# Attention loop of a fused network kernel: the next tile's scores moved directly behind the output products

## The chip, the core and the metric

The kernel runs on one core of a Trainium2 chip. The core has five engines with an instruction stream each, and each runs its stream strictly in the order in which it was written: TensorE (PE, matrix products and transpositions), VectorE (DVE), ScalarE (ACT), GpSimd (POOL) and SyncE (SP, which here issues transfers). They wait for each other through semaphores. The metric is the device time of one execution in microseconds; lower is better. The two levels of TensorE's clock are 1.2 and 2.4 GHz; a granted clock of 1.00 in the profile is 2.4 GHz.

## What is computed

Three layers in a row, all in 32-bit floating point: windowed attention, a mixture of eight experts whose choice of expert runs along the sequence, and a gated two-layer product. Only the first is touched by the change:

```python
def _attn_ref(q, k, v, n_global, n_local):          # (2, 8, 768, 64): batch, heads, sequence, head size
    ...
    scores = scale * np.matmul(q, k.transpose(0, 1, 3, 2))
    keep = is_global | is_local                      # 8 first keys, and the last 96
    scores = np.where(keep, scores + bias[None, :, :, :], -1000000000.0)
    a = np.exp(scores - np.max(scores, axis=-1, keepdims=True))
    a = a / (np.sum(a, axis=-1, keepdims=True) + 1e-09)
    return np.matmul(a, v)
```

The attention output x then meets a small matrix (512 x 9) that gives the routing logits; from them comes, token by token, an expert, and the token's place in that expert's rows.

## The kernel before

**Tiles and iterations.** Attention goes over 12 tiles of 128 queries (6 for each of the two batches), all 8 heads at a time. A tile t is two iterations i = 2t + g of the loop at line 1149, one for each half g of the heads (four heads, as two pairs). A query tile meets 232 keys (128 of its own, 96 before them, 8 global ones); the first tile of a batch meets only its own 128. The order in which the statements stand in the loop is the order on every engine: there is no scheduler.

**The steps of one half i**, with the names by which the text calls them:

- *turns of k and q* (`turn4`, line 854, called by `emit_kT` and `emit_qT`): TensorE transposes the next tile's keys and queries (4 + 4 transpositions) into the two `S` banks; ScalarE evicts them at L862 (into `strip`, a part of the tile `zbig`) and at L866 (into `qz`). Once for each tile, in its even iteration.
- *scores* (`emit_S`, L900): TensorE multiplies `qz` and `strip`. Both halves of tile t + 1 are done in the odd iteration of tile t. The even half goes into the two `S` banks, the odd half into the banks `T` and `O`.
- *minimum* (`emit_min`, L914): VectorE adds the bias table, writes the result into one of the buffers `peb` and takes the row's minimum, four instructions for each half.
- *exponentials* (`emit_exp`, L926): ScalarE, four for each half, in place in `peb`.
- *probability transposes* (`emit_pT`, L933 and L935): TensorE, eight for each half, four into each of the two `PT` banks.
- their *evictions* (`emit_ev`): the first bank by VectorE (L944), the second by ScalarE (L942).
- *output products* (`emit_pv`, L958): both halves of a tile together at the end of the next even iteration, into an `O` bank.
- *x transposes* (`emit_xT`, L963, ScalarE, then `turn_x`, L185, TensorE, then `route_x`, L189, VectorE): the finished tile's output is turned back into rows and scaled.

**The order before.** An odd iteration has on TensorE: probability transposes of the half before, scores of both halves of the next tile, x transposes. An even iteration has: probability transposes of the half before, turns of k and q, output products.

**Routing** goes through the loop in groups of two tiles, by a table `plan` filled by `at(iteration, point, step)` and emptied by `do(i, point)`. The points lie, in the order before: `Ra` behind the probability transposes, `Dm` before the scores, `Rb` behind the x transposes or the turns of k and q, `Db` behind the minimum, `Rc` and `Dc` behind the output products. The steps that the text speaks of are TensorE's *logits* (L203 to L211, and L223 for turning them), *rows* (L263: four transpositions of the tile `ab` that VectorE makes with the chain L228 to L253), *turn* (L282, behind a scan on VectorE, L274), *sum* (L299 and L303), and the two ranking products L347 and L367. Later in the loop the first expert's weights are split in halves by ScalarE (L659) and VectorE (L664) from two points of each iteration, both named `bg_early`.

**Banks.** `S`, `O` and `PT` have two banks each, `T` and `R` one.

Behind the loop come one last half, expert 0 whose products fill TensorE while routing ends, the experts 1 to 7, and the third layer.

Of the kernel before, what the change touches and what calls it, by code (L numbers as in the profile page):

```python
# [9 lines left out]
F32 = mybir.dt.float32  # L10
# [7 lines left out]
P = 128  # L18
B, H, S, HD = 2, 8, 768, 64
D, E, F = 512, 8, 1024  # L20
NT = S // P
NTT = B * NT
# [27 lines left out]
NI = 2 * NTT  # L50
# [6 lines left out]
class Net:  # L57
# [121 lines left out]
        self.slow = c.tile([1, 1], F32, name="slow1")  # L179
        nc.vector.tensor_reduce(self.slow, slow, axis=AX.X, op=ALU.max)  # L180

    def turn_x(self, xT, t):
        self.xp = self.bank("PT", 2)
        for kk in range(KD):
            self.nc.tensor.transpose(self.xp[:, kk * P:(kk + 1) * P], xT[:, kk, :], self.ident)  # L185

# [424 lines left out]
def build(ctx, tc, ins, out):  # L611
    n = Net(ctx, tc, ins, out)
# [241 lines left out]
    def turn4(src):  # L854
        ps = n.bank("S", 2)
        for p in range(PAIRS):
            nc.tensor.transpose(ps[:, p * P:(p + 1) * P], src[:, 2 * p:2 * p + 2, :].rearrange("p a d -> p (a d)"), n.ident)
        return ps.rearrange("p (a c) -> p a c", a=PAIRS)

    def emit_kT(t):  # L860
        psv = turn4(kn.pop(t))
        nc.scalar.activation(out=strip[:, :, cols(t):cols(t) + P], in_=psv, func=ACTF.Copy)  # L862

    def emit_qT(t):
        psv = turn4(qn.pop(t))
        nc.scalar.activation(out=qz[t % 2], in_=psv, func=ACTF.Copy, scale=-1.0 / HD ** 0.5)  # L866

    def first_half(g):
# [35 lines left out]
    def emit_min(i):  # L904
        t, g = divmod(i, 2)
        N = width(t)
        if g == 0:
            stat[t] = (ap.tile([P, H], F32, tag="nm", bufs=3, name=f"nm{t}"), ap.tile([P, H], F32, tag="sm", bufs=3, name=f"sm{t}"))
        tb = n.tb if t % NT else n.tb0
        for b in range(2):  # L910
            for a in range(2):
                h = 4 * g + 2 * b + a
                pe = peb[(4 * i + 2 * b + a) % len(peb)]
                nc.vector.tensor_tensor_reduce(out=pe[:, 2 * P - N:2 * P], in0=Ss[i][a][:, b * N:(b + 1) * N], in1=tb[:, h, :], scale=1.0,  # L914
                                               scalar=3.0e38, op0=ALU.add, op1=ALU.min, accum_out=stat[t][0][:, h:h + 1])
                Pt[i, b, a] = pe
        del Ss[i]
# [81 lines left out]
    def at(i, point, *fs):  # L999
        plan.setdefault((i, point), []).extend(fs)  # L1000

    def do(i, point):
        for f in plan.pop((i, point), ()):
            f()
# [8 lines left out]
    for g in groups:  # L1013
        i = 2 * g[-1] + 3
        lgg, mx, mx2, rows, scan, tn, oh, sm_, ps_, acc = (lambda f=f, g=g: f(ap2, g) for f in (
            lambda _, g: n.route_lgt(ap2, g, xTs), n.route_max, n.route_max2, n.route_rows, n.route_scan, n.route_turn, n.route_oh, n.route_sum,
            lambda _, g: pos(g), n.route_acc))
        if g[-1] == NTT - 1:
            tail = mx, mx2, rows, scan, tn, oh, sm_, ps_
            continue  # L1020
        at(i, "Rb", lgg)
        at(i + 1, "E0", lambda g=g: n.route_lge(ap2, g))
        at(i + 1, "Rb", lambda g=g: n.route_lgb(ap2, g))
        at(i + 1, "Db", mx, mx2)
        if g[-1] == NTT - 3:
            tail8 = rows, scan, tn, oh, sm_, ps_, acc
            continue
        at(i + 1, "Rc", rows)
        if g[-1] == NTT - 5:
            at(i + 1, "Dc", scan)  # L1030
            at(i + 2, "Ra", tn)
            at(i + 2, "Dm", oh)
            at(i + 2, "Rb", sm_)
            at(i + 2, "Db", ps_, acc)
        else:
            at(i + 2, "Dm", scan)
            at(i + 2, "Rb", tn)
            at(i + 2, "Db", oh)
            at(i + 3, "Rb", sm_)
            at(i + 3, "Db", ps_, acc)  # L1040
        if g[-1] in (5, 7):
            e = g[-1] == 7
            at(i + 3 - e, "Db", lambda e=e: n.order_a(ap2, "fg"[e], n.cnte if e else n.cnt6, n.fvec if e else None))
            if e:
                at(i + 3, "Rb", n.order_k)
                at(i + 3, "Db", lambda: n.order_c(ap2, "g", rp))
            else:
                at(i + 3, "Dc", lambda: n.order_b(ap2, "f", rp))
            at(i + 4, "Ra", lambda e=e: n.early_pick(rp, 3 * e))
            at(i + 4, "Dm", lambda e=e: early_start(3 * e, e))  # L1050

    with tc.manual_schedule():
# [3 lines left out]
            load("q", 0, g)  # L1056
        n.setup()
        peb = [ap.tile([P, 2 * P], F32, name=f"peb{i}") if i % 2 else zflat[:, i // 2, S:S + 2 * P] for i in range(8)]
        qzz = ap.tile([P, 2 * PAIRS * P], F32, name="qz")
        qz = [qzz[:, i * D:(i + 1) * D].rearrange("p (a c) -> p a c", a=PAIRS) for i in range(2)]  # L1060
        glob = ap.tile([P, PAIRS, NG], F32, name="glob")
# [86 lines left out]
        tq.pop(0)()  # L1148
        for i in range(NI - 1):
            t, g = divmod(i, 2)  # L1150
            if 0 < i:
                emit_pT(i - 1, 0)
                emit_pT(i - 1, 1)
            do(i, "Ra")
            emit_exp(i, 0)
            do(i, "E0")
            if 0 < i:
                emit_ev(i - 1, 0)
            if i > 1 and g == 1:
                emit_xT(t - 1)  # L1160
            if 0 < i:
                emit_ev(i - 1, 1, True)
            emit_exp(i, 1)
            if i and g == 0:
                n.route_ri(t - 1, stat[t - 1][1])
            do(i, "Dm")
            bg_early()
            if i == 1:
                n.routing_consts()
            ahead = [] if i and not g else [u for u in (i + 1, i + 2) if u < NI and u // 2 == (i + 1) // 2]  # L1170
            for u in ahead:
                emit_S(u)
            for u in ahead:
                if u // 2 % NT < NT - 1:
                    emit_kglob(u)
            if i == 0:
                emit_kglob(0)
            if scq:
                scatter(scq.pop(0))
            if g == 0 and t + 1 < NTT:  # L1180
                emit_kT(t + 1)
                if t + 2 < NTT:
                    load("k", t + 2)
                emit_qT(t + 1)
                if t + 2 < NTT:
                    load("q", t + 2)
            if g == 1 and i > 1:
                n.turn_x(xTs[t - 1], t - 1)
            do(i, "Rb")
            bg_early()  # L1190
            if i < NI - 2:
                emit_min(i + 1)
            if g == 1 and i > 1:
                if t - 1 == XW[0]:
                    n.xw = wp.tile([P, 2 * D], F32, tag="whi", bufs=9, name="xw")
                n.route_x(ap, X, t - 1)
            do(i, "Db")
            for u in (i - 2, i - 1) if i and not g else ():
                emit_pv(u, 0)
                emit_pv(u, 1)  # L1200
            do(i, "Rc")
            do(i, "Dc")
            for _ in scq[:2]:
                scatter(scq.pop(0))
            if g == 1 and t + 2 < NTT:
                load("v", t + 2)
            if g == 0 and 0 < t and (t + 1) % NT and t + 1 < NTT:
                load_vp(t + 1)
            if 0 < i <= E // 2:
                for e in (2 * i - 2, 2 * i - 1):  # L1210
                    nc.scalar.dma_start(out=n.xs[e * REG:e * REG + PRE, :], in_=n.warm)
            if tq:
                for _ in range(NTAB[i]):
                    if tq:
                        tq.pop(0)()
                if not tq:
                    tstack.close()
                    n.counters(ap)
                    dp = astack.enter_context(tc.tile_pool(name="dp", bufs=1, reuse_waits="tile"))
                    dwa = dp.tile([P, 1024], F32, name="dwa")  # L1220
            if i == 3:
                n.gate_rest()
                n.mix_load()
            if i == 4:
                n.mix_rest()
                n.limits(n.const)
            if 0 in wsrc and early is None:
                early = True
                ld_q = list(range(4))
                hi_q = [None] * 3 + [(c, s_) for c in range(NIN) for s_ in range(2)]  # L1230
                bg_early()
            if i in (4, 11, 17):
                dec_load(PIECES[(4, 11, 17).index(i)], dwa)
            if i in (7, 13):
                dgen = dec(PIECES[i // 13], word_tile)
            if i in (7, 8, 9, 13, 14, 15):
                next(dgen, None)
            if i == NI - 2:
                dec_load(PIECES[3], qzz)
# [11 lines left out]
        i = NI - 1  # L1251
# [44 lines left out]
        g = groups[-1]  # L1296
# [710 lines left out]
```

## Time and profile before

| what | before |
|---|---|
| time, median of 3 runs (lowest, highest) | 482.1 us (479.89, 483.13) |
| the profiled execution | 480.05 us, of which 478.2 us are the span from the first to the last instruction |
| granted TensorE clock, mean over the span | 0.999 |
| busy in the span: TensorE, VectorE, ScalarE, GpSimd | 461.2, 344.4, 266.8, 116.4 us |
| the loop's steady part, from tile 1 to tile 11 | 16.78 to 100.67 us, 83.89 us |

In the rows below a time is counted from the start of the span. A matmul's row gives its start, its modelled length, engine, line, out<-in, shape and count; in brackets stand the idle time ahead of it and what ended that. Matmuls overlap: one of 128 columns is shown as 0.27 us long, and the next can start 0.11 us after it started. So a pause on TensorE is read from starts.

### The profile page before, as it was taken

The page shows a single profiled execution, that of the slowest core. Times are in us where ns is not written, and L with a number is a line of the kernel's source. Part 1 is how long each engine was busy: PE and PEld are TensorE (multiplying, and loading weights), DVE is VectorE, ACT ScalarE, POOL GpSimd, SP SyncE. Part 2 cuts the span into 40 slices and gives each one's busy share as a digit, 9 for nine tenths or more (in the row PEclk, how much of TensorE's full clock was granted, in tenths as well). Part 3 has the DMA queues.
Part 4 walks back from the last instruction along what each step waited for, and adds up shares of the span by engine and source line. Part 5 has one row for each costly group of instructions (what it writes and reads, how often), then busy time and mean ns, then how long its engine had stood idle before and what let it go on. Part 6 is the DMA issues. An engine that isn't in the chain of part 4 may idle for free. (4 is left out here: it accounts for less than half of the span.)

```text
span 478.2 us, 9266 instructions
## 1 busy us (share of the span) xinstructions
PE 461.2 (96%) x3210; PEld 396.0 (83%) x3210; DVE 344.4 (72%) x911; ACT 266.8 (56%) x657; POOL 116.4 (24%) x200
## 2 busy tenths in 40 slices
PE   7999999999999999999999999999999999999995
PEld 5787878777788989879879877897989898898984
DVE  6868797896858866987898888797848767363301
ACT  4877877984427735567686686852424324152320
POOL 4112202202300000000010013061844819162220
PEclk9999999999999999999999999999999999999999
DMA  8986486796576886698699743003737451200001
GB/s 193 281 221 165 129 197 185 226 282 217 184 259 203 315 276 253 219 334 311 220 356 377 246 149 111 23 1 118 280 111 265 144 177 53 88 1 23 23 3 49
DMA packets 76491, 86.90 MB, mean 182 GB/s; under 512 B 50676, under 2 KB 50932, under 8 KB 76436
## 3 DMA queue, kind: packets, MB, share of 16 engines
q1 hardware_dynamic: 68176, 63.01, 41.7%
q0 software_dynamic: 4944, 17.17, 10.9%
q10 hardware_dynamic: 3316, 6.03, 3.4%
q8 instruction: 28, 0.46, 0.4%
q14 instruction: 27, 0.22, 0.1%
HBM read 73.49 MB, written 12.71 MB: 180 GB/s over the span
## 5 line engine op out<-in xcount | busy, mean ns | idle before, releaser
L659 ACT ACTIVATE whi<-wraw 128x512 fp32r<-128x512 f32 x128 | 72.5, 623 | 6.5 <-ACT yo L778 2.2
L668 DVE TENSOR_TENSOR wlo<-wraw,whi 128x1024 fp32r<-128x1024 f32 x55 | 66.1, 1218 | 2.4 <-ACT whi L659 2.2
L1518 ACT ACTIVATE sq<-S 128x256 f32<-128x256 f32 x48 | 18.5, 385 | 73.1 <-PE S L677 70.9
L675 PE MATMUL S<-xkh,whi 128*128 128x256 f32 x192 | 54.4, 283 | 0.2 <-ACT whi L659 0.2
L1528 POOL TENSOR_TENSOR kl<-sq,kh 128x256 fp32r<-128x256 f32 x40 | 36.5, 922 | 69.7 <-issue 36.6
L677 PE MATMUL S<-xkh,wlo 128*128 128x256 f32 x192 | 53.3, 277 | 0.2 <-DVE wlo L664 0.2
L676 PE MATMUL S<-xkl,whi 128*128 128x256 f32 x192 | 53.2, 277 | 0.0
L1558 DVE TENSOR_TENSOR o<-O,sig 128x512 f32<-128x512 f32 (+1 forms) x13 | 8.4, 650 | 51.0 <-PE O L677 31.8
L676 PE MATMUL O<-wlo,kh 128*128 128x512 f32 (+1 forms) x104 | 39.2, 377 | 0.6 <-DVE wlo L664 0.6
L677 PE MATMUL O<-whi,kl 128*128 128x512 f32 (+1 forms) x104 | 39.2, 377 | 0.0
L675 PE MATMUL O<-whi,kh 128*128 128x512 f32 (+1 forms) x104 | 38.8, 373 | 0.0
L675 PEld LDWEIGHTS S<-xkh,whi 128*128 128x128 f32 x192 | 36.1, 188 | 0.8 <-ACT whi L659 0.4
L677 PEld LDWEIGHTS S<-xkh,wlo 128*128 128x128 f32 x192 | 36.1, 188 | 0.4 <-DVE wlo L664 0.4
L676 PEld LDWEIGHTS S<-xkl,whi 128*128 128x128 f32 x192 | 36.1, 188 | 0.2
L1519 DVE SCALAR_TENSOR_TENSOR sq<-S,sq 128x256 f32<-128x256 f32 x48 | 20.1, 421 | 15.8 <-ACT sq L1518 15.5
L1527 ACT ACTIVATE kh<-sq 128x256 fp32r<-128x256 f32 x48 | 19.7, 412 | 12.9 <-DVE sq L1519 12.9
L676 PEld LDWEIGHTS O<-wlo,kh 128*128 128x128 f32 x104 | 19.6, 188 | 4.9 <-DVE wlo L664 1.0
L926 ACT ACTIVATE zbig<-zbig,nm 128x232 f32<-128x232 f32 (+1 forms) x48 | 22.4, 466 | 1.7 <-DVE nm L914 0.9
L675 PEld LDWEIGHTS O<-whi,kh 128*128 128x128 f32 x104 | 19.6, 188 | 3.7
L677 PEld LDWEIGHTS O<-whi,kl 128*128 128x128 f32 x104 | 19.6, 188 | 3.5 <-DVE kl L1528 0.2
L926 ACT ACTIVATE peb<-peb,nm 128x232 f32<-128x232 f32 (+1 forms) x48 | 22.2, 464 | 0.0
L307 POOL DMA_INDIRECT xs<-X,posi x10 | 11.4, 1143 | 36.8 <-DVE acc L325 16.7
(466 smaller groups left out, 1407.1 us busy)
## 6 DMA issues: line engine op xcount, KB each, us to landing
wraw<-in_moe_w_dram SPq DMA_DIRECT2D x64, 512.0 KB, 5.3
dwt<-in_moe_w_v_dram POOLq DMA_DIRECT2D x8, 512.0 KB, 4.6
z<-in_moe_w_k_dram SPq DMA_DIRECT2D x8, 512.0 KB, 4.1
z<-in_moe_w_v_dram SPq DMA_DIRECT2D x8, 512.0 KB, 5.0
ys<-yo ACTq DMA_DIRECT2D x13, 256.0 KB, 7.7
vn<-in_v_dram SPq DMA_DIRECT2D x12, 256.0 KB, 3.8
xn<-xs SPq DMA_DIRECT2D x12, 256.0 KB, 4.7
dwt<-in_moe_w_k_dram POOLq DMA_DIRECT2D x6, 512.0 KB, 6.7
```

The source lines that it names most:

```text
L307: self.nc.gpsimd.indirect_dma_start(self.xviews[t], bass.IndirectOffsetOnAxis(ap=self.posi[:, t:t + 1], axis=0), X[t], None)
L659: nc.scalar.activation(out=whl[r, c][0][:, sl], in_=raws[r, c][:, sl], func=ACTF.Copy)
L668: nc.vector.tensor_tensor(lo, raws.pop((r, c)), hi.bitcast(F32), op=ALU.subtract)
L675: nc.tensor.matmul(out_, lhsT=ah, rhs=bh, start=first, stop=False)
L676: nc.tensor.matmul(out_, lhsT=ah, rhs=bl, start=False, stop=False)
L677: nc.tensor.matmul(out_, lhsT=al, rhs=bh, start=False, stop=last)
L926: nc.scalar.activation(out=pe, in_=pe, func=ACTF.Exp, scale=-1.0, bias=nm[:, h:h + 1], accum_out=sm[:, h:h + 1])
L1518: nc.scalar.activation(out=sq_, in_=ps[:, 0:TB], func=ACTF.Relu)
L1519: nc.vector.scalar_tensor_tensor(sq_, ps[:, 0:TB], 0.0, sq_, op0=ALU.max, op1=ALU.mult)
L1527: nc.scalar.activation(out=hh, in_=sq_, func=ACTF.Copy)
L1528: (nc.gpsimd if b else nc.vector).tensor_tensor(hl, sq_, hh.bitcast(F32), op=ALU.subtract)
L1558: nc.vector.tensor_tensor(o[:, a:z], ps[:, 0:z - a], sig[b, i][:, a:z], op=ALU.mult)
```

## The change

- The iterations behind the first tile whose g is 1 (`late`) have another order. The scores of the next tile now stand first, directly behind the output products that end the iteration before. ScalarE's eviction of x and the exponentials follow, the routing point `Ra`, then the probability transposes, then the x transposes; VectorE's minimum stands ahead of the point `Dm` and of the evictions.
- The even iterations put the turns of k and q ahead of the probability transposes (`turned`). Their evictions by ScalarE stay behind the exponentials.
- The x transposes go into an `O` bank instead of a `PT` bank, except in the last odd iteration.
- `peb` has twelve buffers instead of eight, so that the even halves of odd tiles have four of their own; the four new ones lie in the two tiles `exh` and `exl` and are cleared at their edge by four more GpSimd memsets (L1079).
- The routing step *rows* moves from behind the output products (`Rc` of i + 1) to `Ra` of the iteration behind it, for all groups but the one that ends with tile 7.

The first rows are TensorE's, from the end of the output products of tile 4 on. Names: `O_909` and `O_915` are the bank of these products, `S_`, `T_` and `O_962`, `O_939` take the scores of tile 6, `R_` is the routing bank, `PT_` the bank of the probability transposes. Before:

```order
L958 MATMUL O_909<-pt_1_866,vp 64x128 x2
L263 MATMUL R_926<-ident,ab_899 1x128 x4
L933 MATMUL PT_933<-ident,zbig 128x128
...
L935 MATMUL PT_938<-ident,peb_106 128x128
L900 MATMUL S_955<-zbig,qz 128x128
...
L900 MATMUL O_962<-zbig,qz 128x128
L185 MATMUL PT_971<-ident,xT_947 128x128 x4
L282 MATMUL R_976<-ones_r,er_953 128x8 x2
L933 MATMUL PT_991<-ident,zbig 128x128
```

With the change, from the same products on:

```order
L958 MATMUL O_915<-pt_1_880,vp 64x128 x2
L900 MATMUL S_932<-zbig,qz 128x128
...
L900 MATMUL O_939<-zbig,qz 128x128
L263 MATMUL R_954<-ident,ab_905 1x128 x4
L933 MATMUL PT_961<-ident,peexh 128x128
...
L935 MATMUL PT_966<-ident,peexl 128x128
L185 MATMUL O_971<-ident,xT_948 128x128 x4
L282 MATMUL R_988<-ones_r,er_982 128x8 x2
L857 MATMUL S_997<-ident,kn_889 128x128 x4
L857 MATMUL S_1002<-ident,qn_892 128x128 x4
L933 MATMUL PT_1007<-ident,zbig 128x128
```

The scores moved from behind eight probability transposes (and behind *rows*) to directly behind the output products, *rows* and the probability transposes follow them, and the turns of k and q (L857) now stand ahead of the next probability transposes instead of behind them.

The second place is ScalarE in the even iteration that belongs to these products. Before:

```order
L218 ACTIVATE lgt_862<-R_830 128x256
L942 ACTIVATE pt_1_866<-PT_855 128x512
L926 ACTIVATE zbig,sm_840<-zbig,nm_839 128x232
L926 ACTIVATE peb_106,sm_840<-peb_106,nm_839 128x232
L862 ACTIVATE zbig<-S_872 128x4x128
L866 ACTIVATE qz<-S_880 128x512
L266 ACTIVATE br_931<-R_926 1x256
```

With the change:

```order
L218 ACTIVATE lgt_878<-R_842 128x256
L942 ACTIVATE pt_1_882<-PT_871 128x512
L926 ACTIVATE peexl,sm_833<-peexl,nm_832 128x232 x2
L862 ACTIVATE zbig<-S_856 128x4x128
L866 ACTIVATE qz<-S_861 128x512
L963 ACTIVATE xT_948<-O_915 128x512
```

Up to the eviction into `qz` nothing moved here: the eviction of the second `PT` bank (L942), two exponentials, `strip`, `qz`. Behind it the eviction of x (L963) now comes first.

The diff:

```diff
@@ -179,8 +179,8 @@
         self.slow = c.tile([1, 1], F32, name="slow1")
         nc.vector.tensor_reduce(self.slow, slow, axis=AX.X, op=ALU.max)
 
-    def turn_x(self, xT, t):
-        self.xp = self.bank("PT", 2)
+    def turn_x(self, xT, t, tag="PT"):
+        self.xp = self.bank(tag, 2)
         for kk in range(KD):
             self.nc.tensor.transpose(self.xp[:, kk * P:(kk + 1) * P], xT[:, kk, :], self.ident)
 
@@ -857,12 +857,12 @@
             nc.tensor.transpose(ps[:, p * P:(p + 1) * P], src[:, 2 * p:2 * p + 2, :].rearrange("p a d -> p (a d)"), n.ident)
         return ps.rearrange("p (a c) -> p a c", a=PAIRS)
 
-    def emit_kT(t):
-        psv = turn4(kn.pop(t))
+    def emit_kT(t, psv=None):
+        psv = turn4(kn.pop(t)) if psv is None else psv
         nc.scalar.activation(out=strip[:, :, cols(t):cols(t) + P], in_=psv, func=ACTF.Copy)
 
-    def emit_qT(t):
-        psv = turn4(qn.pop(t))
+    def emit_qT(t, psv=None):
+        psv = turn4(qn.pop(t)) if psv is None else psv
         nc.scalar.activation(out=qz[t % 2], in_=psv, func=ACTF.Copy, scale=-1.0 / HD ** 0.5)
 
     def first_half(g):
@@ -910,7 +910,7 @@
         for b in range(2):
             for a in range(2):
                 h = 4 * g + 2 * b + a
-                pe = peb[(4 * i + 2 * b + a) % len(peb)]
+                pe = peb[4 * (1 if g else t % 2 * 2) + 2 * b + a]
                 nc.vector.tensor_tensor_reduce(out=pe[:, 2 * P - N:2 * P], in0=Ss[i][a][:, b * N:(b + 1) * N], in1=tb[:, h, :], scale=1.0,
                                                scalar=3.0e38, op0=ALU.add, op1=ALU.min, accum_out=stat[t][0][:, h:h + 1])
                 Pt[i, b, a] = pe
@@ -1025,14 +1025,15 @@
         if g[-1] == NTT - 3:
             tail8 = rows, scan, tn, oh, sm_, ps_, acc
             continue
-        at(i + 1, "Rc", rows)
         if g[-1] == NTT - 5:
+            at(i + 1, "Rc", rows)
             at(i + 1, "Dc", scan)
             at(i + 2, "Ra", tn)
             at(i + 2, "Dm", oh)
             at(i + 2, "Rb", sm_)
             at(i + 2, "Db", ps_, acc)
         else:
+            at(i + 2, "Ra", rows)
             at(i + 2, "Dm", scan)
             at(i + 2, "Rb", tn)
             at(i + 2, "Db", oh)
@@ -1056,6 +1057,9 @@
             load("q", 0, g)
         n.setup()
         peb = [ap.tile([P, 2 * P], F32, name=f"peb{i}") if i % 2 else zflat[:, i // 2, S:S + 2 * P] for i in range(8)]
+        for tg in ("exh", "exl"):
+            more = ap.tile([P, 4 * P], F32, tag=tg, bufs=2, name="pe" + tg)
+            peb += [more[:, 0:2 * P], more[:, 2 * P:4 * P]]
         qzz = ap.tile([P, 2 * PAIRS * P], F32, name="qz")
         qz = [qzz[:, i * D:(i + 1) * D].rearrange("p (a c) -> p a c", a=PAIRS) for i in range(2)]
         glob = ap.tile([P, PAIRS, NG], F32, name="glob")
@@ -1148,49 +1152,68 @@
         tq.pop(0)()
         for i in range(NI - 1):
             t, g = divmod(i, 2)
-            if 0 < i:
+            late = g == 1 and i > 1
+            ahead = [] if i and not g else [u for u in (i + 1, i + 2) if u < NI and u // 2 == (i + 1) // 2]
+
+            def scores():
+                for u in ahead:
+                    emit_S(u)
+                for u in ahead:
+                    if u // 2 % NT < NT - 1:
+                        emit_kglob(u)
+                if i == 0:
+                    emit_kglob(0)
+
+            turned = []
+            if late:
+                scores()
+                emit_xT(t - 1)
+                emit_exp(i, 0)
+                emit_exp(i, 1)
+                do(i, "Ra")
                 emit_pT(i - 1, 0)
                 emit_pT(i - 1, 1)
-            do(i, "Ra")
-            emit_exp(i, 0)
-            do(i, "E0")
-            if 0 < i:
+                n.turn_x(xTs[t - 1], t - 1, "O" if i < NI - 3 else "PT")
+                if i < NI - 2:
+                    emit_min(i + 1)
+                do(i, "Dm")
                 emit_ev(i - 1, 0)
-            if i > 1 and g == 1:
-                emit_xT(t - 1)
-            if 0 < i:
                 emit_ev(i - 1, 1, True)
-            emit_exp(i, 1)
-            if i and g == 0:
-                n.route_ri(t - 1, stat[t - 1][1])
-            do(i, "Dm")
+            else:
+                if i and t + 1 < NTT and not g:
+                    turned = [turn4(kn.pop(t + 1)), turn4(qn.pop(t + 1))]
+                if 0 < i:
+                    emit_pT(i - 1, 0)
+                    emit_pT(i - 1, 1)
+                do(i, "Ra")
+                emit_exp(i, 0)
+                do(i, "E0")
+                if 0 < i:
+                    emit_ev(i - 1, 0)
+                    emit_ev(i - 1, 1, True)
+                emit_exp(i, 1)
+                if i and g == 0:
+                    n.route_ri(t - 1, stat[t - 1][1])
+                do(i, "Dm")
             bg_early()
             if i == 1:
                 n.routing_consts()
-            ahead = [] if i and not g else [u for u in (i + 1, i + 2) if u < NI and u // 2 == (i + 1) // 2]
-            for u in ahead:
-                emit_S(u)
-            for u in ahead:
-                if u // 2 % NT < NT - 1:
-                    emit_kglob(u)
-            if i == 0:
-                emit_kglob(0)
+            if not late:
+                scores()
             if scq:
                 scatter(scq.pop(0))
             if g == 0 and t + 1 < NTT:
-                emit_kT(t + 1)
+                emit_kT(t + 1, *turned[0:1])
                 if t + 2 < NTT:
                     load("k", t + 2)
-                emit_qT(t + 1)
+                emit_qT(t + 1, *turned[1:2])
                 if t + 2 < NTT:
                     load("q", t + 2)
-            if g == 1 and i > 1:
-                n.turn_x(xTs[t - 1], t - 1)
             do(i, "Rb")
             bg_early()
-            if i < NI - 2:
+            if i < NI - 2 and not late:
                 emit_min(i + 1)
-            if g == 1 and i > 1:
+            if late:
                 if t - 1 == XW[0]:
                     n.xw = wp.tile([P, 2 * D], F32, tag="whi", bufs=9, name="xw")
                 n.route_x(ap, X, t - 1)
```

## Rows read from the trace of the kernel before

**Rows 1.** Stages: us, length, busy time (count) of each engine, granted clock, DMA share, GB/s

```profile
16.78:100.67 83.89, 79.51 (x885) 66.36 (x884) 68.30 (x313) 68.73 (x225) 15.45 (x34) 1.00 0.75 202
100.67:478.20 377.53, 368.17 (x2241) 320.19 (x2239) 263.32 (x522) 188.22 (x399) 93.82 (x123) 1.00 0.51 176
90.00:100.00 10.00, 8.99 (x115) 7.30 (x114) 9.83 (x37) 9.38 (x30) 2.59 (x3) 1.00 0.66 207
```

**Rows 2.** Waits of TensorE, 13 to 101 us: idle us in total, times, longest

```profile
PE PT L933 <- DVE X L189: 1.3, 3, 0.5
PE R L367 <- ACT peb L926: 0.7, 1, 0.7
PE R L263 <- DVE eq L239: 0.6, 1, 0.6
PE R L263 <- DVE ab L253: 0.5, 2, 0.3
PE R L263 <- DVE ab L242: 0.4, 2, 0.2
PE R L282 <- DVE er L274: 0.4, 1, 0.4
PE R L347 <- DVE dgf L339: 0.2, 1, 0.2
```

**Rows 3.** Timeline of TensorE over a tile without routing steps

```profile
16.78 0.33 PE L933 MATMUL PT<-ident,zbig 128*128 128x128 f32 x1
...
17.80 1.05 PE L900 MATMUL S<-zbig,qz 64*128 64x232 f32 x8
...
19.57 0.66 PE L185 MATMUL PT<-ident,xT 128*128 128x128 f32 x4
...
21.47 0.27 PE L935 MATMUL PT<-ident,peb 128*128 128x128 f32 x1
21.58 0.60 PE L857 MATMUL S<-ident,kn 128*128 128x128 f32 x4
...
22.55 0.44 PE L958 MATMUL O<-pt,vn 128*64 128x128 f32 x4
...
24.45 0.33 PE L933 MATMUL PT<-ident,zbig 128*128 128x128 f32 x1
```

**Rows 4.** Timeline of ScalarE over the same tile

```profile
21.84 0.60 ACT L942 ACTIVATE pt<-PT 128x512 f32<-128x512 f32 x1 [0.96 <-PE PT L935]
...
23.76 0.59 ACT L866 ACTIVATE qz<-S 128x512 f32<-128x512 f32 x1
```

**Rows 5.** Timeline of ScalarE and TensorE at the first scores of tile 1

```profile
11.00 0.60 ACT L866 ACTIVATE qz<-S 128x512 f32<-128x512 f32 x1
...
11.74 1.05 PE L900 MATMUL S<-zbig,qz 64*128 64x232 f32 x8 [0.41 <-ACT qz L866]
```

**Rows 6.** Timeline of TensorE: *sum*, turned logits, and the output products behind them

```profile
63.66 1.09 PE L958 MATMUL O<-pt,vn 128*64 128x128 f32 x16
...
71.78 0.26 PE L299 MATMUL R<-OH,tri 128*128 128x16 f32 x1
...
72.41 0.44 PE L958 MATMUL O<-pt,vn 128*64 128x128 f32 x4
...
80.54 0.38 PE L223 MATMUL R<-ident,lgt 128*128 128x128 f32 x2
80.86 0.44 PE L958 MATMUL O<-pt,vn 128*64 128x128 f32 x4
```

**Rows 7.** Timeline of TensorE: the step behind *rows*, after the products of 80.86

```profile
83.72 0.27 PE L933 MATMUL PT<-ident,zbig 128*128 128x128 f32 x1
```

**Rows 8.** Timeline of ScalarE: a weight split ahead of the evictions of k and q

```profile
90.90 0.62 ACT L659 ACTIVATE whi<-wraw 128x512 fp32r<-128x512 f32 x1
```

**Rows 9.** Timeline of TensorE: the turns of k and q of tile 2

```profile
14.52 0.66 PE L857 MATMUL S<-ident,kn 128*128 128x128 f32 x4 [0.35 <-DVE nm L914]
```

**Rows 10.** Timeline of GpSimd: its step behind the memsets of L1079

```profile
5.85 0.32 POOL L593 TENSOR_SCALAR tb<-d 128x128 f32<-128x128 f32 x1 [2.31 <-DVE d L584]
```

## Prediction

> **What bounds the kernel now.** I read the busy time by stage first. In the loop's steady part, 16.78 to 100.67 us, TensorE is busy for 79.51 of 83.89 us, VectorE and ScalarE for 68.3 and 68.7; behind it TensorE is busy for 368.17 of 377.53 us; the granted clock is 1.00, the 2.4 GHz level, in both [rows 1]. So TensorE bounds the loop and all that follows, and a microsecond won or lost on it in the loop should reach the end.
>
> Next I read what TensorE waits for in the loop. The idle time sums to 4.1 us over 11 waits [rows 2]: probability transposes wait for VectorE's reading of the x transposes, with which they share the `PT` banks (1.3); *rows* waits for the logits' chain (0.6 + 0.5 + 0.4); the ranking products L367 and L347 wait for VectorE's ranking (0.7, put down to ScalarE there, and 0.2); *turn* waits for the scan (0.4). The view counts from a matmul's modelled end, 0.27 us behind its start, while the next can start 0.11 us behind it (21.47, 21.58) [rows 3]. So each wait loses about 0.16 us more than is listed. That is all the change can win in the loop.
>
> Last I read one tile without routing on TensorE and ScalarE [rows 3, 4]. TensorE: transposes 16.78, scores 17.80, x transposes 19.57, last probability transposition 21.47, turns of k and q 21.58, products 22.55, next tile 24.45. ScalarE: it starts to evict the second `PT` bank at 21.84, then does two exponentials, then k, and ends the eviction into `qz` at 23.76 + 0.59 = 24.35. Now look at what comes first at 24.45: probability transposes, which need none of it. The scores that read `qz` start a further 17.80 - 16.78 = 1.02 us later. This order hides the eviction.
>
> **What the change removes.** Waits: two of the three on the `PT` banks (the third is in the last odd iteration, which keeps that bank), some 0.9 idle + 2 x 0.16 = 1.2 us. The *rows* waits of three groups: five waits, 1.5 + 5 x 0.16 = 2.3 us, less the 0.5 of the group that ends with tile 7, which stays: its products start at 80.86, take 1.90 (22.55 to 24.45 [rows 3]), the four transpositions need 0.44, and yet the next step is at 83.72, not 83.20 [rows 6, 7]. So 1.8 us. Now the scores (17.80 to 19.57, 1.77 us [rows 3]) stand ahead of *rows*, L367 and *turn*, and hide what VectorE still has to do. L367 gives 0.7 + 0.05, *turn* 0.4. Sum 4.15 us. Waits shorter than 0.16 us cannot show in that view; with up to one for each of the ten tiles that is 0 to 1.6 us, of which I take the middle, 0.8. **Removed: 5.0 us.** Nothing is computed less: the count of products, evictions and exponentials is the same.
>
> **What it adds: a wait of the scores for `qz`.** Let s be the start of an even iteration's last probability transposition. ScalarE evicts k and q only behind the eviction of that transposition's bank and two exponentials; the written order on ScalarE is the same up to `qz`. So `qz` is ready at s + 24.35 - 21.47 = s + 2.88 [rows 3, 4]. Where TensorE has waited for `qz` the scores started 11.74 - 11.60 = 0.14 us behind its end [rows 5]. With the change the scores start no earlier than s + 3.02. What else has TensorE from s on? The turns of k and q now lie ahead of s. There remain 0.11, the routing step at `Rb`, and the products, 1.90: without routing it arrives at s + 2.05, with the turned logits (80.54 to 80.86, 0.32) at s + 2.37, with *sum* (71.78 to 72.41, 0.63) at s + 2.69 [rows 6]. It waits 0.97, 0.65 or 0.33 us. By iteration:
>
> - i = 4, no routing: 0.97. i = 6 and 10, logits: 1.3 together. i = 8 and 12, *sum*: 0.66 together, of which I take 0.5, since in 12 the exponentials are those of a narrow tile.
> - i = 14, logits, but products of a first tile: 63.66 and 1.09 long, about 0.9 less cover; its bank of transposes is half as wide, and I estimate 0.2 of L942's 0.60 [rows 4] off: 0.65 + 0.9 - 0.2 = 1.3.
> - i = 16 and 18: here L347 and *rows* still stand behind the products and wait for a VectorE chain that starts at the probability transposes. The turns of k and q (0.97 [rows 3]) stood between the two and no longer do, so both waits grow by between 0 and that: *rows*, the longer one, from 0.5 to 1.4; L347, of 0.2 [rows 2], by a little over half, to 0.75. The wait for `qz` runs inside these. Added: 0.55 + 0.9 = 1.45.
> - i = 20: no routing but L347 (0.1), and a weight split of ScalarE stands between the exponentials and k (0.62 long, half a microsecond from start to start) [rows 8]: 0.97 - 0.1 + 0.5 = 1.35.
> - i = 22 turns no k or q: nothing.
>
> Sum: 0.97 + 1.3 + 0.5 + 1.3 + 1.45 + 1.35 = 6.9 us. At the start, i = 2: the turns of k wait for VectorE's minimum in the `S` banks until 14.52 now [rows 9], and would again, though asked for earlier. They take 0.97, four transpositions follow, s is 15.8, and the scores start at s + 3.02 less 0.2 for the narrow bank, 18.6, where the odd iteration began at 16.78: 1.8 us. **Added: 8.7 us.**
>
> A rule bears on this. The Trainium skill, Perfetto Trace Analysis, Matmuls, says that product groups should rotate through banks so that the eviction of one lies beside the next group's matmuls. By it nothing is lost here, as transposes and products (2.8 us) lie between the turns of k and q and the scores in both orders, against about 1.1 us of eviction, and the sum would be -5.0. The rows say otherwise: the eviction does not begin when its bank is full, it queues behind work that needs s.
>
> **Costed at nothing.** Four more memsets on GpSimd: behind them it idles 2.31 us for VectorE [rows 10], which hides them; without that they would be four short steps in a row, well under a microsecond. Banks: VectorE's minimum frees `S`, and its reading of x the `O` bank for the products, while TensorE does probability transposes, x transposes and routing, 1.8 us and more (19.57 to 21.47 [rows 3]); were VectorE later than that, the products would wait (rival 3). The order of transfers on SP stays; the first expert's load is issued behind the scores now, 1.77 us later in its iteration, and three slots of `bg_early` lie between it and the first split.
>
> **The sum.** -5.0 + 8.7 = +3.7 us, against the profiled execution's own 480.05: 483.7. The median is 2 us above that execution; with it the same sum gives 485.8. Three runs 3.2 us apart do not say which to take; I put the forecast between, **484.7**.
>
> **Rivals.**
> 1. *Faster: the waits go and none takes their place*, 480.05 - 5.0 to 482.1 - 5.0, 475 to 477. The mechanism: ScalarE evicts k and q while transposes and products run, and is done by s + 2.1, when TensorE arrives. It decides at 0.8 us: if ScalarE's chain from s to `qz` were that much shorter than 2.88. For it: ScalarE idled 0.96 us ahead of that chain [rows 4], so it does not lag. Against: the idling ends with the transposes, and the chain is in order behind them. The Trainium skill, Perfetto Trace Analysis, Optimization Strategy, says that the same gap repeating may mean too few buffers. The waits on `PT` agree: three, 1.3 us [rows 2].
> 2. *No change, 480 to 483*: half the new wait is given back. TensorE idles 9.4 us behind the loop [rows 1]; where weights or routing set that, a later loop end meets inputs that are further ahead, and VectorE, 98% busy from 90 to 100 us, catches up while TensorE waits. For it: these numbers. Against: 9.4 us idle in 377 leave little to give back.
> 3. *Slower still, 488 to 492*: VectorE falls behind in the last iterations. It was 9.83 of 10 us busy [rows 1], and minimum and scan now go ahead of the eviction that frees `PT`. From a lag of 1 us on, each of the last four tiles would lose 1 to 2 us more.
>
> **How the numbers follow.** The forecast, slower by 1.5 to 6 us, gets 0.60 (481.5 to 487.5); rival 1 0.10; rival 2 0.17; rival 3 0.13. A measurement of this kernel can tell about 1%, 4.8 us, from no change. Faster by more than that: rival 1, 0.10. Slower: rival 3 and the upper third of the forecast, 0.13 + 0.19 = 0.32. Within 1%: 0.58. The range, 480.5 to 489, leaves out rival 1 and the outer ends of rivals 2 and 3.
>
> **What would show it.** In the new profile scores (L900) wait for ScalarE's `qz`, about 0.3 to 1.3 us in nearly every tile, and the waits of L263 (but one group), L282 and of L933 for x are gone. From the last probability transposition to the scores it is 3.0 us. The loop's steady part ends near 104 us, and the rest is as long as before. The forecast is wrong if the scores follow the products at once, if the loop's end moves less than 1.5 us, or if VectorE is what the waits name.

## The result and the profile after

The change makes the kernel slower by a little: 483.54 us median against 480.35 us, twelve runs each, a ratio of 1.0059 (95% interval 1.0034 to 1.0084), or +2.8 us by that ratio. The prediction was 484.7, 2.6 us above the 482.1 that was known then. The profiled execution took 482.91 us with a span of 481.0, 2.8 more than before.

The stages first, as in [rows 1] (columns as there; the loop now begins with the scores at 17.91 and ends at 103.42):

```profile
17.91:103.42 85.51, 77.60 (x884) 66.96 (x884) 68.00 (x308) 68.76 (x225) 15.45 (x34) 1.00 0.73 197
103.42:481.00 377.58, 367.51 (x2241) 320.31 (x2239) 263.40 (x522) 187.69 (x398) 93.67 (x123) 1.00 0.51 175
90.00:100.00 10.00, 8.38 (x101) 7.06 (x99) 9.21 (x40) 9.48 (x28) 3.04 (x3) 1.00 0.51 165
```

The loop's end moved from 100.67 to 103.42, by 2.75 us; what lies behind it is as long as it was (377.58 against 377.53). In the last tiles VectorE is less full than before (9.21 of 10 us against 9.83).

What TensorE waits for, 13 to 106 us, beside [rows 2] (idle us, times, longest):

```profile
PE S L900 <- issue: 5.9, 7, 1.4
PE R L263 <- DVE ab L242: 1.0, 1, 1.0
PE R L347 <- DVE dgf L339: 0.8, 1, 0.8
PE S L857 <- DVE nm L914: 0.8, 1, 0.8
PE PT L185 <- DVE pt L944: 0.4, 1, 0.4
PE R L263 <- DVE ab L253: 0.3, 1, 0.3
PE S L900 <- ACT qz L866: 0.2, 1, 0.2
```

The waits of L933 for x, of L282 and of L367 are gone, and of L263 two are left. What stands in their place is above all the wait of the scores L900; L347 and L263 (at 85.20 us) have grown behind the products, as has that of the turns L857 for VectorE's minimum. The view puts nearly all of the wait of L900 down to "issue", that is, to nothing that it knows. The timelines tell more. TensorE in the first tile without routing, then ScalarE (as in [rows 3, 4]; s is 22.68):

```profile
22.68 0.27 PE L935 MATMUL PT<-ident,peb 128*128 128x128 f32 x1
22.88 0.44 PE L958 MATMUL O<-pt,vn 128*64 128x128 f32 x4
...
25.65 0.47 PE L900 MATMUL S<-zbig,qz 64*128 64x232 f32 x2 [0.80 <-issue]
```

```profile
23.05 0.60 ACT L942 ACTIVATE pt<-PT 128x512 f32<-128x512 f32 x1 [0.31 <-PE PT L935]
...
23.54 0.48 ACT L926 ACTIVATE zbig<-zbig,nm 128x232 f32<-128x232 f32 x1
...
24.49 0.58 ACT L862 ACTIVATE zbig<-S 128x512 f32<-128x512 f32 x1
24.96 0.59 ACT L866 ACTIVATE qz<-S 128x512 f32<-128x512 f32 x1
```

`qz` is ready at 24.96 + 0.59 = 25.55, s + 2.87, and the scores start at 25.65, s + 2.97. The prediction had 2.88 and 3.02.

### The profile page after: what moved, and what is told of

It reads as the page before. It is cut to its first block, busy times and chain, and to the rows that moved or that the text cites. A ratio compares the mean times of both kernels' runs of the same rounds, so it can differ in the third digit from the quotient of the medians.

```text
span 481.0 us, 9252 instructions
## 1 busy us (share of the span) xinstructions
PE 457.8 (95%) x3210; PEld 396.4 (82%) x3210; DVE 345.3 (72%) x911; ACT 266.8 (55%) x657; POOL 116.4 (24%) x204
## 5 line engine op out<-in xcount | busy, mean ns | idle before, releaser
L942 ACT ACTIVATE pt<-PT 128x512 f32<-128x512 f32 (+1 forms) x24 | 13.5, 561 | 16.3 <-PE PT L935 13.7
L944 DVE COPY pt<-PT 128x512 f32<-128x512 f32 (+1 forms) x24 | 15.3, 639 | 5.9 <-PE PT L935 4.7
```

Source lines behind the costliest of these rows:

```text
L942: nc.scalar.activation(out=d[:, 0:ps.shape[1]], in_=ps, func=ACTF.Copy)
L944: nc.vector.tensor_copy(d[:, 0:ps.shape[1]], ps)
```

## The experiments

Beside the ratio each kernel has the length of its loop in the trace, since 1 us is near the limit of what the ratios can tell: from the start of the first scores of 16 products (i = 1) to the first transposition behind the last products of the loop. Before the change that is 11.74 to 100.67, 88.93 us. Each length is from one execution, so a few tenths of a microsecond between two of them show little; e3, e7 and e8 began late, which shortens their first tile (see e3 and the last section).

| kernel | loop, us | against before | ratio to before (95%) |
|---|---|---|---|
| changed | 92.12 | +3.19 | 1.0059 (1.0034 to 1.0084) |
| e1_evict_first | 89.15 | +0.22 | 0.998 (0.9959 to 1.0001) |
| e2_turns_behind | 86.83 | -2.10 | 0.9947 (0.9919 to 0.9975) |
| e3_both | 85.23 | -3.70 | 0.9938 (0.9912 to 0.9963) |
| e4_banks_rows | 87.96 | -0.97 | 0.9965 (0.994 to 0.999) |
| e4o_bank_only | 88.29 | -0.64 | 0.998 (0.996 to 0.9999) |
| e5_both_tail | 86.47 | -2.46 | 0.9963 (0.9943 to 0.9983) |
| e6_rows_back | 90.02 | +1.09 | 1.0025 (1.0006 to 1.0045) |
| e7_bank_back | 92.33 | +3.40 | 1.0063 (1.0041 to 1.0085) |
| e8_scores_behind_pT | 90.50 | +1.57 | 1.004 (1.0013 to 1.0068) |

The theory: the scores wait for `qz`, which queues on ScalarE behind an eviction and two exponentials. The rivals: they wait for something else; or the wait, once taken away here, turns up on VectorE.

### e1: evict k and q ahead of two exponentials

```diff
                     emit_ev(i - 1, 1, True)
+                if turned:
+                    emit_kT(t + 1, turned[0])
+                    emit_qT(t + 1, turned[1])
                 emit_exp(i, 1)
```

> The changed kernel with one edit: in the even iterations ScalarE evicts k and q (L862, L866) directly behind the eviction of the second transposed bank, ahead of the two exponentials of i instead of behind them. The turns on TensorE stay where the change put them. Theory (scores wait for qz, which queues on ScalarE): two exponentials are 0.95 us from start to start, so qz ends at s + 1.9 instead of s + 2.9 and the scores can start at s + 2.1. The wait of L900 behind the products (0.8, 0.6, 0.5 us in i = 4, 6, 8, 1.3 in i = 14, 1.2 in i = 20, and the 1.1 that the first odd iteration comes late) falls by up to 0.95 each, 5 us in all; the loop's steady part then ends near 98 us and the kernel is 2 to 3 us faster than before the change (ratio to the kernel before about 0.995). Rival (the scores wait for something else, such as the reading of the S banks by VectorE's minimum or the matmul queue itself, which the view calls issue): scores still start 3.0 us behind s, ratio about 1.006. Rival (the wait only moves): the exponentials, now 1.1 us later, hold back the probability transpositions behind the scores; ratio about 1.00 to 1.006 and the wait stands at L933.

The same tile, TensorE and then ScalarE:

```profile
21.31 0.27 PE L935 MATMUL PT<-ident,peb 128*128 128x128 f32 x1
...
23.45 0.47 PE L900 MATMUL S<-zbig,qz 64*128 64x232 f32 x2
```

```profile
22.76 0.59 ACT L866 ACTIVATE qz<-S 128x512 f32<-128x512 f32 x1
```

`qz` ends 2.04 us behind s, the scores start at s + 2.14, right behind the products, and no wait stands on them in this tile; 0.8 us of it is left in the two tiles with short products (16.54 and 62.97). So it was `qz`, whatever the view named, and no wait stands at L933, where the third theory had it. The loop is 2.97 us shorter than that of the changed kernel, though, and not 5, and the ratio 0.998 instead of 0.995. What went missing is named by the waits of e1:

```profile
PE R L282 <- DVE er L274: 1.1, 2, 0.8
PE R L263 <- DVE ab L242: 1.0, 1, 1.0
PE S L857 <- DVE nm L914: 0.9, 1, 0.9
PE R L347 <- DVE dgf L339: 0.8, 1, 0.8
PE S L900 <- issue: 0.8, 2, 0.5
```

From the scores of tile 8 to those of tile 9 (issued in i = 15 and 17) e1 takes 10.09 us, the changed kernel 9.20: L282 now waits 0.82 us at 67.47 for VectorE's scan, which ran until 67.41. Another 0.86 is lost from the last scores on, 0.46 of it inside them: they take from 90.83 to 93.12 (95.19 to 97.02 in the changed kernel), and go on in the banks `T` and `O` at 92.08, when VectorE's minimum has read these until 92.02. Here the wait for `qz` had been hiding VectorE.

### e2: the turns of k and q behind the probability transpositions again

```diff
-                if i and t + 1 < NTT and not g:
-                    turned = [turn4(kn.pop(t + 1)), turn4(qn.pop(t + 1))]
```

> The changed kernel with one edit: in the even iterations the turns of k and q stand behind the probability transpositions again, as before the change; all other parts stay, ScalarE's order too. Theory: qz still ends 2.9 us behind s, but s comes 0.97 us earlier, since the turns now lie between s and the products, so TensorE arrives at s + 3.0 and the wait goes: 5 us less than the changed kernel, and also the about 1.4 us by which L347 (i = 16) and the rows step (i = 18) grew: 476 to 478 for this chip's 480 before, ratio to the kernel before 0.992 to 0.996. Rival (moving the scores is what costs, and not the turns): ratio about 1.006 as the changed kernel. Rival (turns ahead hide the exponentials' lateness): a new wait of 0.3 to 1 us per tile at L933 in even iterations and a ratio near 1.00.

This one step in the order is worth 5.29 us of loop against the changed kernel, and takes it from slower to faster than before; 6.4 were expected. TensorE in the same tile, and the first of the waits:

```profile
20.34 0.27 PE L935 MATMUL PT<-ident,peb 128*128 128x128 f32 x1
20.45 0.60 PE L857 MATMUL S<-ident,kn 128*128 128x128 f32 x4
...
23.61 0.47 PE L900 MATMUL S<-zbig,qz 64*128 64x232 f32 x2 [0.22 <-ACT qz L866]
```

```profile
PE S L900 <- ACT qz L866: 1.9, 4, 0.9
PE R L347 <- DVE dgf L339: 0.6, 1, 0.6
...
PE PT L933 <- DVE pt L944: 0.2, 1, 0.2
```

The scores start at s + 3.27, with the 0.97 us of turns between s and the products as cover; 1.9 us of the wait is left in four places, now under its own name. Of new waits L933 has a single one of 0.2 us, so the third theory of its expectation falls.

### e3: both edits

> The changed kernel with both edits: turns of k and q behind the probability transpositions, and ScalarE evicts k and q ahead of the second pair of exponentials. Theory: qz ends at s + 1.9, TensorE arrives at s + 3.0, so that also the two tiles with less cover (i = 14, with short products, and i = 20, with a weight split of ScalarE in between) wait no more: 1 to 2 us less than with the turns moved back alone, ratio to the kernel before 0.988 to 0.994. Rival (VectorE is next, 92 to 98% busy from 90 to 100 us): no better than either edit alone.

The wait of L900 is gone altogether, and this kernel has the lowest median, 477.59 us, and the lowest ratio, 0.9938; its interval overlaps that of e2, so only the trace tells the two apart. Its waits begin with VectorE's ranking and its last tiles:

```profile
PE R L347 <- DVE dgf L339: 0.7, 1, 0.7
PE PT L185 <- DVE pt L944: 0.6, 1, 0.6
PE R L282 <- DVE er L274: 0.3, 1, 0.3
```

Its loop began late in the profiled execution (see the last section), which shortens its first tile: 4.62 us from the first scores of 16 products to the next, 5.03 in e5, which has the same order there. Without that 0.41 its loop would be some 85.6 us, 1.2 less than that of e2, within the 1 to 2 expected.

### e4 and e4o: the bank and the rows step alone, in the old order

```diff
-        self.xp = self.bank("PT", 2)
+        self.xp = self.bank(tag, 2)
...
-                n.turn_x(xTs[t - 1], t - 1)
+                n.turn_x(xTs[t - 1], t - 1, "O" if i < NI - 3 else "PT")
```

and, in e4 alone,

```diff
-        at(i + 1, "Rc", rows)
         if g[-1] == NTT - 5:
+            at(i + 1, "Rc", rows)
...
         else:
+            at(i + 2, "Ra", rows)
```

> The kernel before with two parts of the change alone: the turn of x goes into an O bank (but in the last odd iteration), and the rows step of the routing moves into the next odd iteration, behind its probability transpositions; the order of scores and turns stays as before, and so do the eight probability buffers. Theory (these parts are worth what their waits were): the two waits of L933 for VectorE's reading of x go (1.2 us) and four of the five waits of L263 (1.8 us): ratio to the kernel before about 0.994, loop's steady part ending near 97.7 us. Rival (the waits were only where VectorE's lateness showed, and the next step waits instead): ratio 1.00, and the waits stand at L263, L282 or at the products L958.

> The kernel before with one part of the change alone: the turn of x goes into an O bank (but in the last odd iteration). With the rows step moved as well, e4_banks_rows won 1.0 us of the loop (from the first scores of 16 products to the loop's end) where 3.0 were expected, and its trace had a new wait of 1.1 us for ScalarE's eviction into xT, behind an eviction of the rows step that now stands ahead of the exponentials on ScalarE and made it idle 2.4 us. Theory (the two parts are worth their waits, and the moved rows step cost 1 us of that through ScalarE's order): the bank alone wins its two waits, 1.2 us, ratio 0.997 to 0.998, no wait for xT. Rival (the bank itself makes xT and the products wait): ratio 1.00, with waits at L185 or L958.

Together they win 0.97 us, not 3.0, and the bank alone 0.64, not 1.2. The largest of the waits of e4, the place of its longest one, and ScalarE just ahead of it:

```profile
PE O L185 <- ACT xT L963: 1.1, 2, 0.8
```

```profile
51.93 0.33 PE L185 MATMUL O<-ident,xT 128*128 128x128 f32 x1 [0.79 <-ACT xT L963]
```

```profile
50.08 0.37 ACT L266 ACTIVATE br<-R 1x256 f32<-1x256 f32 x1 [2.36 <-PE R L263]
```

In the old order the rows step, put at that place, stands ahead of ScalarE's exponentials, and its eviction L266 makes ScalarE idle 2.36 us there (7.2 us in all its four places, 6.0 before). In e4o the wait for `xT` isn't there, but the waits of *rows* for L239 grow from 0.6 [rows 2] to

```profile
PE R L263 <- DVE eq L239: 1.9, 2, 1.2
```

So about half of what the bank was expected to give is taken back one step later, at VectorE's chain.

### e6 and e7: the rows step, or the bank, put back into e2

> e2_turns_behind with the rows step back where the kernel before had it, behind the products of the even iteration and so ahead of the scores. Theory (rows waits for VectorE's chain, and the scores behind which the change puts it hide that wait): the waits of L263 come back, four of 0.2 to 0.6 us with 0.16 each, so 1.8 us more than e2: ratio to the kernel before 0.998 to 0.999. Rival (the scores wait at that place for qz anyway, so that the rows wait lies inside that one): less than 0.7 us more than e2, ratio 0.995.

> e2_turns_behind with the turn of x in a PT bank again, as in the kernel before. Theory (the O bank is needed by the new order, more than in the old one): the turn of x now follows both probability transpositions of the same iteration, which hold both PT banks, and VectorE empties the first only behind four minimums, so it waits about 0.5 to 1.5 us in each of nine tiles: 5 to 12 us more than e2, ratio 1.005 to 1.02. Rival (worth only the two waits that the kernel before showed): 1.2 us more than e2, ratio 0.997.

In e2's order the two parts are worth more than in the old one: 3.19 us (86.83 to 90.02) for the rows step, 5.50 (to 92.33) for the bank. The waits of e6 from 13 us on, and of e7:

```profile
PE S L900 <- ACT qz L866: 2.1, 3, 0.9
PE R L263 <- DVE eq L239: 1.9, 2, 1.2
```

```profile
PE PT L185 <- DVE pt L944: 3.9, 7, 1.1
PE PT L185 <- ACT pt L942: 2.1, 3, 0.8
```

In e7 the turn of x waits for a `PT` bank in ten places, 6.0 us. Without either part the early scores do not pay (1.0025 and 1.0063), and without the early scores the two parts hardly do.

### e5: e3, with the `PT` bank emptied ahead of the last minimum

```diff
-                if i < NI - 2:
+                if i < NI - 3:
                     emit_min(i + 1)
                 do(i, "Dm")
                 emit_ev(i - 1, 0)
+                if i == NI - 3:
+                    emit_min(i + 1)
```

> e3_both with one more edit: in the last odd iteration, where the turn of x keeps a PT bank, VectorE empties that bank ahead of the four minimums instead of behind them. In e3 the turn of x waits there 0.8 us (93.77 to 94.57). Theory: that wait goes and the loop's end comes 0.5 to 0.9 us earlier, ratio to the kernel before 0.992 to 0.993, at the edge of what the comparison resolves, so read from the trace. Rival (VectorE, 9.7 of 10 us busy there, has the same work left): what is gained at the turn of x is lost at the products or the logits behind it, and the loop's length is that of e3.

The theory fell, and the rival was right that the gain would be lost. The loop is even longer (86.47 against 85.23, or 85.6 with e5's start), all of it behind the last scores; the turn of x still waits 0.4 us, and behind it comes

```profile
94.97 0.33 PE L933 MATMUL PT<-ident,zbig 128*128 128x128 f32 x1 [1.20 <-DVE X L189]
```

### e8: the scores behind the probability transpositions again

```diff
             if late:
-                scores()
                 emit_xT(t - 1)
                 emit_exp(i, 0)
                 emit_exp(i, 1)
-                do(i, "Ra")
                 emit_pT(i - 1, 0)
                 emit_pT(i - 1, 1)
+                scores()
+                do(i, "Ra")
```

> The changed kernel with one edit: in the odd iterations the eight probability transpositions stand ahead of the next tile's scores again (and the rows step behind the scores); the turns of k and q stay ahead of the probability transpositions of the even iteration. Theory (the wait needs both moves: the turns ahead of s and nothing between the products and the scores): with the 1.0 us of probability transpositions in between TensorE arrives at s + 3.1 and waits for qz no more in the tiles with long products, 0.3 us in i = 14 and 20, and the first odd iteration starts 1 us earlier; the growth of L347 (i = 16) and rows (i = 18), 1.5 us, stays. From the first scores of 16 products to the loop's end about 86 to 87 us against 92.1 in the changed kernel and 86.8 with the turns moved back; ratio to the kernel before 0.993 to 0.997. Rival (the turns ahead are what costs, whatever stands behind): 91 us or more and a ratio above 1.00. Rival (VectorE's evictions, which still stand behind the minimum of these scores, now hold both PT banks longer): waits of 0.3 to 1 us per tile at the probability transpositions, 88 to 91 us.

The wait for `qz` is down to 0.7 us here too, as the theory has it, but the loop is 90.50 us, as the third theory had it (88 to 91), and the ratio 1.004, as the second had it (above 1.00). The waits stand at other places than the third named:

```profile
PE R L282 <- DVE er L274: 2.3, 3, 0.8
PE PT L185 <- ACT pt L942: 1.3, 1, 1.3
PE R L263 <- DVE ab L242: 1.0, 1, 1.0
```

VectorE in two tiles:

```profile
21.44 0.40 DVE L914 CUSTOM_DVE_ANT_0 zbig<-S,tb 128x232 f32<-128x232 f32 x1 [1.69 <-PE S L900]
...
28.55 0.40 DVE L914 CUSTOM_DVE_ANT_0 peexh<-S,tb 128x232 f32<-128x232 f32 x1 [1.68 <-PE S L900]
```

VectorE, whose order has the minimum ahead of the evictions, stands idle there until the scores come, and is late with the scan afterwards (L282). In these two tiles the changed kernel, whose scores wait for `qz`, has it idle nearly as long, 1.69 and 1.50 us; over the loop it idles so for 9.0 us in eight places in e8, for 5.9 in seven in the changed kernel and for 5.8 in e2. That the early scores pay because they feed VectorE fits this, but no run shows it alone: e8 also keeps the turns ahead, so its second theory is not excluded.

## Why the prediction was right, step by step

**TensorE carries a loss to the end.** Right: +2.75 us at the loop's end, +2.8 in the span, +2.8 by the ratio of the runs. Nothing is given back behind the loop, so rival 2 falls. Rival 3 falls too: from 93 us on the only wait that names VectorE is that of L185, 0.4 us. Ahead of that VectorE is named at L857, L347 and L263, 2.6 us in the three places where the prediction had it (i = 2, 16 and 18); it takes more only where the wait for `qz` is taken off (e1, e8).

**The new wait.** Its mechanism is shown by e1 (ScalarE's order alone takes 6.1 us of it down to 0.8) and by e2 (TensorE's order alone, to 1.9). Its sizes, as the time from the last product's start to the scores, less the 0.21 us that this step takes in e3 without a wait:

| i | 4 | 6 | 8 | 10 | 12 | 14 | 20 | sum |
|---|---|---|---|---|---|---|---|---|
| predicted, us | 0.97 | 0.65 | 0.33 | 0.65 | 0.17 | 1.3 | 1.35 | 5.4 |
| measured, us | 0.86 | 0.64 | 0.57 | 0.27 | 0.23 | 1.35 | 1.25 | 5.2 |

In i = 8 and 10 they are off by +0.24 and -0.38, which nearly cancels, by luck: in i = 8 *sum* adds 0.30 us to TensorE's path and not the 0.63 read from a later one, and in i = 10 the products themselves pause 0.27 us (49.34 to 49.83) for VectorE's eviction L944, which ran until 49.77. The prediction's s + 2.05 is a small slip too, 0.11 + 1.90 being 2.01; e1 has 2.14 without a wait. The two large ones came as worked out, i = 14 from its short products and i = 20 from the weight split between the exponentials and k. The two waits that stay behind the products grew as well: L347 (i = 16) by 0.66 (0.55 predicted), *rows* (i = 18) by 0.86 (0.9). The start lost 1.57 us (from the scores of i = 1 to the begin of i = 3, 5.04 before, 6.61 now) where 1.8 were predicted. Added: 5.2 + 0.7 + 0.9 + 1.6 = 8.3 us; predicted 8.7.

What was costed at nothing cost nothing: GpSimd's step behind the memsets starts at 5.85 us in both kernels.

The Trainium skill, Perfetto Trace Analysis, Matmuls, would have product groups rotate through banks so that one's eviction lies beside the next one's matmuls. The trace agrees only in part: with q's eviction at 22.76 (e1) nothing waits in this tile, but in the changed kernel the last transposition into q's bank started at 21.81, its eviction only at 24.96, and the scores waited.

**What was removed.** By difference, and only so, 8.3 - 3.2 = 5.1 us, predicted 5.0. The sum is right, but not the way it was put together: the parts are no addends. The bank was put at 1.2 and is worth 0.64 alone and 5.50 in e2's order; bank and rows were put at 3.0 and are worth 0.97 together in the old order; the rows step, put at 1.8, is worth 3.19 in e2's. The prediction did have the early scores hide the wait of *rows*, which e4 lacks; but it took the parts one by one. That the removed waits had one cause, VectorE being late, and go together only when the scores feed it earlier, fits e4 to e8 and is argued, since no run made VectorE alone faster. That the parts came to 5.0 was in part luck, the more so as 0.8 of it was the middle of a range of 0 to 1.6.

**Rival 1** had its condition right: with k and q evicted by s + 2.0 (e1) the scores wait in two tiles only, 0.8 us. Its price was too good. It gave 475 to 477, and e1 is at 480.06, since VectorE's scan and ranking wait next; even e3, without any wait for `qz`, stays 1.3 us of loop (1.7 with e5's start) short of the full 5.0 (L347, L282 and the last tiles).

**The forecast time**, 484.7, was put between two bases 2 us apart, since three runs could not tell which to take; that it came within 1.2 us is in part luck. On the profiled execution alone it was 483.7, nearer to the 483.54 that was measured: the 482.1 of three runs lay 1.8 above the median of twelve.

## What to carry to other kernels

When a consumer is moved forward on one engine, count from the event that starts its producer's chain, and include what is queued ahead on the producer's engine: here 1.1 us of evicting was done only at s + 2.9, because the eviction of another bank and two exponentials came first. Move the work that starts the chain along with it, or put it ahead in that queue: moving the turns back took the change from +0.6% to -0.5%. And do not add up waits that may have one cause: two parts of this change, put into the old order, won a third of what their waits were.

## What the runs showed of the hardware

**The pace at the start varies between executions.** In the profiled execution of e3 the matmuls of the first tile went at half their usual pace. TensorE, and its window (columns as in [rows 1]):

```profile
13.32 0.42 PE L933 MATMUL PT<-ident,peb 128*128 128x128 f32 x1
13.53 0.42 PE L933 MATMUL PT<-ident,zbig 128*128 128x128 f32 x1
...
14.09 1.05 PE L900 MATMUL S<-zbig,qz 64*128 64x232 f32 x8
```

```profile
7.00:14.00 7.00, 6.08 (x32) 4.99 (x32) 4.97 (x29) 3.93 (x14) 1.85 (x15) 1.00 0.93 190
```

They are 0.21 us apart and 0.42 long, elsewhere 0.11 and 0.27, and the first scores of 16 products start at 14.09, against 10.78 in e2. The granted clock of 1.00 in that row is not a reading: the trace's records of the clock, at 1.00, begin only at 13.90 us in e3, and the view prints 1.00 where there is none. In e7 they begin at 14.56 and in e8 at 14.33, in the eight other traces between 4.4 and 6.6 us, and where the pace changes it does so there: in e7 the scores go on at the usual pace from 14.61. Half the pace is what the lower of the two levels, 1.2 GHz, would give; that TensorE was at it is inferred from the pace, not recorded. The loops of e7 and e8 begin at 14.10 and 14.09 as well; the others between 10.77 and 11.74. The runs of one kernel lie up to 6.7 us apart (e8, 481.52 to 488.19); such a start, some 3.3 us later, could explain a part of that. What sets it was not tried. It is why loops are compared from their first scores here.

**"issue" as a releaser does not mean that nothing was waited for.** The wait for `qz` is put down to it in seven places of the changed kernel (5.9 us), and to `qz` by name in an eighth (0.2) and in e2, where it is the same wait.
